# Channel attention and a rational feed-forward layer on one core: numerator in SBUF, whole-tile tail steps, output turned by VectorE

## The chip, the cores and the metric

The kernel runs on one core of a Trainium2 chip. The metric is the device time of one execution in microseconds (us). The engines are named as in the profile: PE is TensorE (matmuls; PEld is its weight load), DVE is VectorE, ACT is ScalarE, POOL is GpSimd, and SP is SyncE, which issues the DMAs. SBUF is the on-chip working memory, PSUM the small memory into which PE writes.

## The reference

Two layers in float32, with B = 4, N = 6080, C = 256 and F = 2048:

```python
qn = q / (norm(q, axis=1) + 1e-6); kn = k / (norm(k, axis=1) + 1e-6)
s = kn.T @ qn / tau                      # 256 x 256 for each batch
a = softmax(s, axis=-1)
x = (v @ a).reshape(24320, 256)
h = x @ w_in                             # 24320 x 2048
P = a0 + a1*h + a2*h**2 + a3*h**3
Q = 1 + abs(b0)*abs(h) + abs(b1)*h**2
out = (P / (Q + 1e-6)) @ w_out           # 24320 x 256
```

## The kernel before, in words

**Tiling.** The 6080 rows of a batch are cut into 12 groups: eleven of 512 rows and one of 448, so 48 groups in all, 44 full ones and 4 of 448. Counted by rows they are 47.5 full groups. The attention matrix is folded into `w_in` once for each batch (`Attn.fuse`), so that a group is `v` times eight weight pieces. The 2048 hidden channels are eight *pairs* of 128, so one group is eight calls of `pair`, and a pair's tile is 128 partitions by 2 x 512 = 1024 float32 elements.

**One pair.** PE computes h into `hx`, a PSUM tile of two banks (three such tiles exist), from high and low float32r parts of `v` and of the weight. Then, in SBUF tiles `d`, `r`, `uu` (names `y` and `kk` in the code):

- the denominator Q goes to `d`. A pair of the form F (lines 804 to 810) takes one ACT step, one DVE step `prod`, another ACT step, and later a POOL step `one` that adds 1. The form U (811 to 823) takes two ACT steps and two POOL steps, `line` and `sum`;
- ACT makes `slope` (826), DVE makes `num1` (828) and `num2` (830). `num2` writes the numerator without a0 **back into `hx` in PSUM**;
- ACT makes `root` (834) and `square` (839), which give r = 1/Q approximately;
- the *tail* runs in two halves of 512 elements (852 to 882). DVE `quot` forms (hx + a0)·r, POOL `again` multiplies it by Q in `d`. In an S pair DVE `last` makes the corrected quotient `g`, which PE multiplies with `w_out` in float32. In an R pair DVE `rest` forms the remainder, POOL `last_pool` turns it into a low part `gl`, and PE multiplies high and low parts in float32r.

In each of the DVE steps `prod`, `num1`, `num2`, `quot`, `rest` and `last`, one of the two tensor operands lies in PSUM (`hx`).

`KIND` (line 51) names the form of each of the eight pairs: the first letter is R or S, the second F or U, the third (P) puts the last step of an R pair on POOL. Before, four pairs are R and four are S.

**One group.** All eight pairs add into one PSUM tile `acc`. `finish` (884) copies it with ACT, turns it with eight PE transposes back into `acc`, copies again with ACT into `orow`, and stores it with one DMA. `values` (740) loads `v` with one DMA, turns it on PE, and splits it into `vhi` (ACT) and `vlo` (DVE).

**Order.** `step` does not issue anything: it hands a step with its engine, its cost and a key (from the tables `LAG` and `TIME`) to `Planner`. The planner plays the schedule through with these costs and emits every engine's instructions in the order that it found. Each engine then runs its queue strictly in that order. The planner knows an argument `port`: a DVE step that carries it, and every POOL step, are taken one after the other. `Attn` gives that argument to its DVE steps on the sums of squares, and `piece` to its late weight steps; `pair` gives it to none.

Beside the groups, the next batch's q and k rows are squared by ACT into `sq` and summed by POOL into `ssq` (24 pieces to a batch), and multiplied on PE.

Of the kernel before, what the change touches and what calls it, by code (L numbers as in the profile page):

```python
# [10 lines left out]
F32 = mybir.dt.float32  # L11
# [9 lines left out]
LAG = {  # L21
    "first": (-23.943, 0.779, 16.152, -2.628, 12.275, -14.299, 0.849, 12.204),
    "second": (64.578, 55.323, 59.143, 56.607, 7.413, 49.338, 52.686, 69.362),
    "line": (11.809, -44.33, -0.798, -23.493, 7.232, -28.691, -20.654, -32.78),
    "prod": (-25.799, -25.066, -7.177, -0.027, 1.503, -30.754, -29.951, -14.021),
    "abs": (22.851, -16.828, -6.381, 4.349, 3.845, 0.375, -1.748, -5.521),
    "slope": (-2.413, -14.175, 23.292, -11.592, 10.064, 22.358, 14.327, 33.823),
    "num1": (102.929, 82.894, 81.158, 62.614, 64.142, 120.209, 89.073, 104.516),
    "num2": (-4.828, -66.826, -23.076, -34.364, -51.549, -56.374, -41.833, -65.959),
    "sum": (4.693, 16.192, 3.118, 9.167, 1.798, 5.734, -2.218, 21.491),  # L30
    "root": (8.815, 1.931, -7.534, -8.44, 11.521, 1.596, -18.294, 11.215),
    "one": (27.21, 31.412, 40.487, 22.316, 24.471, -12.593, 43.293, 5.876),
    "square": (-64.503, -49.599, -58.591, -28.542, -47.268, -42.996, -32.677, -8.585),
    "quot": (40.746, 32.008, 16.16, 51.527, 29.306, 35.7, 39.709, 24.527),
    "again": (-61.355, -87.995, -84.935, -58.616, -91.448, -79.4, -44.502, -69.519),
    "rest": (-17.013, -33.435, -9.224, -61.671, -10.183, -41.213, -23.935, -25.063),
    "last": (-39.442, -40.174, -68.15, -83.691, -21.902, -24.741, -46.676, -44.956),
    "last_pool": (-0.493, -59.623, -7.515, -32.037, 18.764, -45.886, -12.678, -10.454),
    "out": (63.96, 25.995, 31.164, 31.971, 24.821, 19.268, 27.921, 33.051),
    "out_lo": (116.352, 93.718, 68.074, 61.654, 91.315, 121.222, 76.822, 102.449),  # L40
}
TIME = {
    "pair": 6.5, "start": 92.588, "load": 1.191, "softmax": 58.031, "in": 2.437,
    "late_in": -22.444, "out0": -54.096, "out": 7.105, "attn0_0": 31.018, "attn_0": 1.206,
    "attn0": 69.854, "attn": 0.995, "attn1": 94.156, "value": 1.073, "fuse": 5.271,
    "finish": -40.738, "front": 35.456, "front_pace": 13.309, "back": 50.586, "store": 55.554,
    "ahead_pe": 283.994, "ahead_act": 1891641.487, "ahead_dve": 6393007968.0, "ahead_pool": 11581445.34,
# [3 lines left out]
KIND = ("RFP", "SU", "RFP", "SF", "RFP", "SU", "RFP", "SF")  # L51
# [63 lines left out]
class Planner:  # L115
# [5 lines left out]
    HOP = {"PE": 0.25, "ACT": 0.07, "DVE": 0.07, "POOL": 0.07, "SP": 3.5}  # L121
# [39 lines left out]
    def order(self):  # L161
# [55 lines left out]
        while left:  # L217
            for e in ready:
                while busy[e] <= now and ready[e]:
# [55 lines left out]
def tile_channel_attention_rational_ffn(  # L275
# [41 lines left out]
    def apart(eng, ins):  # L317
# [4 lines left out]
        slot, bank = half[0]  # L322
        for other, old in seen.get((slot, 1 - bank), ()):
            if other is not eng:
                tc.declare_no_dep(ins.ins, old.ins, reason="the two use different banks of one tile")
        mine = seen.setdefault((slot, bank), [])
        mine.append((eng, ins))
# [79 lines left out]
    b0, b1 = babs[:, 0:1], babs[:, 1:2]  # L407
    w_in_sb = const.tile([P, NC2, F], F32, name="w_in_sb")
# [331 lines left out]
    def values(G, at, gate=()):  # L740
        b, g = divmod(G, NG)
        base, pn = groups[g]
        n = T * pn
        vst = buf("vst", [P, T, C], F32)
        slot = banks()
        hi, lo = buf("vhi", [P, NC2, GT], F32R), buf("vlo", [P, NC2, GT], F32R)
        fn = lambda: sp.dma_start(vst[:pn], v[b, base : base + pn * T].rearrange("(p t) c -> p t c", t=T))
        step("SP", 1.5, at - 3 * II, fn, gate, [vst])

        def turned():  # L750
            for c in range(NC2):
                for t in range(T):
                    pe.transpose(
                        slot[:, c, t * pn : (t + 1) * pn], vst[:pn, t, c * P : (c + 1) * P], ident[:pn, :pn]
                    )
# [10 lines left out]
    def pair(m, at, vparts, w, acc):  # L766
# [23 lines left out]
        for i in range(2):  # L790
            step("PE", 1.38 * s, at + 0.01 * i, lambda i=i: mm1(i), [whi, wlo, vhi, vlo], [hx.both[i]])

        def mm2(i, w, x, first, last):
            for a, g in zip(w, x):
                for e in range(NC2):
                    pe.matmul(
                        acc[:, e, :n], a[:, W_AT[p] + i, e * P : (e + 1) * P], g[:, :n],
                        start=(first and a is w[0]), stop=(last and a is w[-1]),
                    )
# [4 lines left out]
        if kind[1] == "F":  # L804
            fn = lambda: act.activation(c(kk), c(hx), AF.Abs, scale=b1)
            step("ACT", cost(0.87, 0.25), at + LAG["first"][p], fn, [hx], [kk], rank=at + 1.0)
            fn = lambda: dve.scalar_tensor_tensor(c(d), c(kk), b0, c(hx), op0=ALU.add, op1=ALU.mult)
            step("DVE", cost(1.06, 0.22), at + LAG["prod"][p], fn, [kk, hx], [d], rank=at + 1.0)
            fn = lambda: act.activation(c(d), c(d), AF.Abs)
            step("ACT", cost(0.87, 0.17), at + LAG["abs"][p], fn, [d], [d])  # L810
        else:
            fn = lambda: act.activation(c(d), c(hx), AF.Square)
            step("ACT", cost(0.87, 0.16), at + LAG["first"][p], fn, [hx], [d], rank=at + 1.0)
            fn = lambda: act.activation(c(kk), c(hx), AF.Abs, scale=b0)
            step("ACT", cost(0.87, 0.25), at + LAG["second"][p], fn, [hx], [kk], rank=at + 1.0)
            if kind[1] == "A":
                fn = lambda: act.activation(c(d), c(d), AF.Identity, scale=b1, bias=ONE)
                step("ACT", cost(0.87, 0.27), at + LAG["line"][p], fn, [d], [d])
            else:
                fn = lambda: pool.tensor_scalar(c(d), c(d), b1, ONE, op0=ALU.mult, op1=ALU.add)  # L820
                step("POOL", cost(1.06, 0.07), at + LAG["line"][p], fn, [d], [d])
            fn = lambda: pool.tensor_tensor(c(d), c(d), c(kk), op=ALU.add)
# [147 lines left out]
```

## Time and profile before

| | |
|---|---|
| median of 3 runs | 2693.04 us (2691.68 to 2693.2) |
| profiled execution, its own time | 2693.56 us |
| its span, first to last instruction | 2691.8 us |
| mean granted PE clock | 0.992 |
| PE busy | 2601.5 us, 10304 instructions |
| DVE busy | 2473.1 us, 2911 instructions |
| ACT busy | 2238.9 us, 2285 instructions |
| POOL busy | 2287.1 us, 1725 instructions |
| DMA on q1 | 69168 packets, 108.03 MB |

A row of a group of instructions reads: line, engine, operation, output<-inputs with partitions x elements, count | busy us, mean ns of one | idle time before them. Nearly all rows have line 64, since a helper there issues every operation; the tile names tell them apart. A row of a timeline reads: start and duration in us, engine, operation, and in brackets the idle time before it.

### The profile page before, as it was taken

How to read it: one execution, taken by the hardware profiler on the slowest of the kernel's cores; microseconds unless marked ns; L12 is line 12 of the kernel's file. 1: busy time of each engine (PE TensorE's matmuls, PEld its weight loads, DVE VectorE, ACT ScalarE, POOL GpSimd, SP SyncE). 2: the span in 40 equal slices, each digit the busy share in tenths (PEclk: the TensorE clock that was granted, in tenths of full speed). 3: DMA queues.
4: the chain of work that ended last, by engine and by line, in shares of the span. 5: the costliest groups of instructions: out<-in, count | busy, mean ns of one | idle time of the engine just before them, and what ended most of it. 6: DMA issues, size and time to landing. Idle time of an engine off the chain costs nothing.

```text
span 2691.8 us, 30390 instructions
## 1 busy us (share of the span) xinstructions
PE 2601.5 (97%) x10304; PEld 1864.0 (69%) x10304; DVE 2473.1 (92%) x2911; ACT 2238.9 (83%) x2285; POOL 2287.1 (85%) x1725
## 2 busy tenths in 40 slices
PE   7899999999999999999999999999999999999998
PEld 5766667666766666667777667667777666667666
DVE  8889998899979999998888999999888999999998
ACT  5688887788888888888878888888786888898896
POOL 6598888888768888889978898888996898898897
PEclk9899999999999999999999999999999999999999
DMA  9400002000100000012210000001220000000000
GB/s 318 139 18 16 24 16 85 16 16 31 41 22 16 24 24 16 24 40 77 79 60 15 32 15 17 32 16 47 78 77 24 23 8 24 32 8 24 31 9 15
DMA packets 69324, 109.97 MB, mean 41 GB/s; under 512 B 5296, under 2 KB 53936, under 8 KB 69168
## 3 DMA queue, kind: packets, MB, share of 16 engines
q1 hardware_dynamic: 69168, 108.03, 12.0%
q8 instruction: 81, 1.33, 0.2%
q14 instruction: 75, 0.61, 0.1%
HBM read 83.10 MB, written 24.90 MB: 40 GB/s over the span
## 4 chain that ended last, share of the span: by engine, by line
DVE 38%; PE 33%; POOL 11%; issue 8%; ACT 8%; DMA 1%; SPq 0%; DVEq 0%; POOLq 0%; ACTq 0%
PE hx L64 18%; PE acc L64 15%; DVE hx L64 13%; DVE d L64 9%; DVE uu L64 7%; POOL d L64 7%; DVE g L64 4%; DVE gh L64 3%; ACT uu L64 3%; ACT r L64 2%; POOL gl L64 2%; POOL ssq L64 2%; DVE vlo L64 1%; ACT d L64 1%; POOL orow L64 1%
## 5 line engine op out<-in xcount | busy, mean ns | idle before, releaser
L64 PE MATMUL hx<-vhi,w 128*128 128x512 f32 (+1 forms) x3072 | 1094.5, 413 | 42.4 <-DVE g L64 25.1
L64 PEld LDWEIGHTS hx<-vhi,w 128*128 128x128 f32 x3072 | 578.4, 188 | 240.2 <-DVE g L64 51.8
L64 PE MATMUL acc<-g,w_out_sb 128*128 128x512 f32 (+1 forms) x1536 | 688.9, 587 | 1.1 <-DVE g L64 1.1
L64 POOL TENSOR_TENSOR d<-d,gh 128x512 f32<-128x512 f32 (+1 forms) x384 | 484.2, 1282 | 192.4 <-DVE gh L64 191.9
L64 PE MATMUL hx<-vlo,w 128*128 128x512 f32 (+1 forms) x1536 | 598.5, 390 | 0.0
L64 ACT ACTIVATE uu<-hx,babs 128x1024 f32<-128x1024 f32 (+1 forms) x384 | 423.3, 1102 | 164.9 <-PE hx L64 163.1
L64 POOL TENSOR_TENSOR gl<-d,r 128x512 fp32r<-128x512 f32 (+1 forms) x384 | 489.7, 1283 | 19.9 <-DVE d L64 18.7
L64 DVE SCALAR_TENSOR_TENSOR hx<-uu,coef,hx 128x1024 f32<-128x1024 f32 (+1 forms) x384 | 488.9, 1273 | 3.5
L64 POOL TENSOR_TENSOR d<-d,r 128x512 f32<-128x512 f32 (+1 forms) x384 | 481.3, 1276 | 10.6 <-ACT r L64 8.1
L64 DVE TENSOR_TENSOR uu<-uu,hx 128x1024 f32<-128x1024 f32 (+1 forms) x384 | 461.7, 1202 | 27.8 <-ACT uu L64 27.0
L64 PEld LDWEIGHTS acc<-g,w_out_sb 128*128 128x128 f32 x1536 | 289.9, 189 | 273.1 <-issue 254.7
L64 ACT ACTIVATE uu<-hx,coef 128x1024 f32<-128x1024 f32 (+1 forms) x384 | 457.0, 1190 | 0.0
L64 ACT ACTIVATE r<-d 128x1024 f32<-128x1024 f32 (+1 forms) x384 | 401.9, 1047 | 37.6 <-POOL d L64 34.6
L64 ACT ACTIVATE d<-d 128x1024 f32<-128x1024 f32 (+1 forms) x288 | 301.4, 1047 | 140.7 <-DVE d L64 140.3
L64 ACT ACTIVATE r<-r 128x1024 f32<-128x1024 f32 (+1 forms) x384 | 402.2, 1048 | 5.7
L64 DVE SCALAR_TENSOR_TENSOR d<-uu,babs,hx 128x1024 f32<-128x1024 f32 (+1 forms) x288 | 364.2, 1264 | 29.3 <-ACT uu L64 25.9
L64 POOL TENSOR_SCALAR d<-d,ones 128x1024 f32<-128x1024 f32 (+1 forms) x288 | 322.6, 1120 | 78.0 <-ACT r L64 77.1
L64 PEld LDWEIGHTS hx<-vlo,w 128*128 128x128 f32 x1536 | 290.0, 189 | 72.6 <-issue 26.8
L64 DVE SCALAR_TENSOR_TENSOR d<-hx,coef,d 128x512 f32<-128x512 f32 (+1 forms) x384 | 282.9, 741 | 51.8 <-POOL d L64 51.6
L64 DVE SCALAR_TENSOR_TENSOR hx<-hx,coef,r 128x512 f32<-128x512 f32 (+1 forms) x384 | 288.4, 751 | 22.7 <-ACT r L64 13.4
L64 DVE SCALAR_TENSOR_TENSOR gh<-hx,coef,r 128x512 fp32r<-128x512 f32 (+1 forms) x384 | 269.4, 740 | 23.9 <-ACT r L64 15.4
L64 DVE SCALAR_TENSOR_TENSOR g<-d,hx 128x512 f32<-128x512 f32 (+1 forms) x384 | 257.3, 679 | 20.4 <-POOL d L64 6.5
(101 smaller groups left out, 2990.1 us busy)
## 6 DMA issues: line engine op xcount, KB each, us to landing
vst<-in_v_dram SPq DMA_DIRECT2D x44, 512.0 KB, 3.4
out_dram<-orow SPq DMA_DIRECT2D x44, 512.0 KB, 2.6
kq<-in_k_dram SPq DMA_DIRECT2D x78, 256.0 KB, 3.5
kq<-in_q_dram SPq DMA_DIRECT2D x78, 256.0 KB, 3.8
d<-in_moe_w_in_dram SPq DMA_DIRECT2D x8, 512.0 KB, 6.5
r<-in_k_dram SPq DMA_DIRECT2D x10, 256.0 KB, 6.0
r<-in_q_dram SPq DMA_DIRECT2D x10, 256.0 KB, 6.0
d<-in_moe_w_out_dram SPq DMA_DIRECT2D x4, 512.0 KB, 5.7
```

What stands on the lines that cost most here:

```text
L64: ins = op(*args, **kwargs)
```

## The change

- The numerator: `num2` writes into `y` in SBUF and no longer into `hx`. The steps `quot`, `rest` and `last` then read `y`, and `hx` is released after `num2`.
- The tail runs on the whole tile of 1024 elements: one `quot`, one `again`, one `rest` and one `last` or `last_pool` for a pair, where there were two of each.
- The denominator: a pair of the new form G makes |b1|·h² and |b0|·|h| in two ACT steps (the first with a scale of the root of |b1|, worked out once at the start by `square_root`) and adds them and 1 in one DVE step `prod` whose two tensor inputs are `kk` and `d`. The POOL step `one` and the ACT step `abs` go. A pair of the form A has the step `line` on ACT and `sum` on POOL.
- `KIND`: seven of eight pairs are R (five RGP, two RAP) and one is S (SG).
- The output: `finish` turns `acc` from PSUM into `orow` with one DVE block transpose (32 x 32 blocks) and stores it in four DMAs with runs of 32 elements. The two ACT copies and the eight PE transposes go.
- The rows of `v` come in four DMAs and another row order; they are still turned on PE.
- Slots: `uu` 4 to 5, `w` 9 to 8, `gh` 6 halves to 3 whole tiles, `gl` 4 halves to 2 whole tiles, `g` goes. The planner gets finer costs for the step from one engine to another, and other values of `LAG` and `TIME`.

```diff
-KIND = ("RFP", "SU", "RFP", "SF", "RFP", "SU", "RFP", "SF")
+KIND = ("RGP", "RAP", "RGP", "RGP", "RAP", "RGP", "RGP", "SG")
+VIN = "PE"
+VLO = "DVE"
...
-    SLOTS = {"hA": 3, "hB": 3, "acc": 1, "d": 3, "uu": 4, "r": 3, "gh": 6, "gl": 4, "g": 4, "w": 9, ...
+    SLOTS = {"hA": 3, "hB": 3, "acc": 1, "d": 3, "uu": 5, "r": 3, "gh": 3, "gl": 2, "w": 8, ...
...
+        def put(eng, per, fixed, name, fn, reads, writes, rank=None):
+            step(eng, cost(per, fixed), at + LAG[name][p], fn, reads, writes, rank=None if rank is None else at + rank)
...
+        if kind[1] == "G":
+            fn = lambda: act.activation(c(d), c(hx), AF.Square, scale=b1r)
+            put("ACT", 0.87, 0.25, "first", fn, [hx], [d], 1.0)
+            fn = lambda: act.activation(c(kk), c(hx), AF.Abs, scale=b0)
+            put("ACT", 0.87, 0.25, "second", fn, [hx], [kk], 1.0)
+            fn = lambda: dve.scalar_tensor_tensor(c(d), c(kk), ONE, c(d), op0=ALU.add, op1=ALU.add)
+            put("DVE", 1.06, 0.2, "prod", fn, [kk, d], [d])
...
-        fn = lambda: dve.scalar_tensor_tensor(c(hx), c(y), a1, c(hx), op0=ALU.add, op1=ALU.mult)
+        fn = lambda: dve.scalar_tensor_tensor(c(y), c(y), a1, c(hx), op0=ALU.add, op1=ALU.mult)
...
+        if kind[0] == "S":
+            fn = lambda: pool.tensor_tensor(c(d), c(d), c(r), op=ALU.mult)
+            put("POOL", 2.32, 0.06, "again", fn, [d, r], [d])
+            fn = lambda: dve.scalar_tensor_tensor(c(y), c(y), a0, c(r), op0=ALU.add, op1=ALU.mult)
+            put("DVE", 1.06, 0.2, "quot", fn, [y, r], [y])
+            fn = lambda: dve.scalar_tensor_tensor(
+                c(y), c(d), 2.0, c(y), op0=ALU.subtract, op1=ALU.mult, reverse0=True
+            )
+            put("DVE", 1.06, 0.2, "last", fn, [d, y], [y])
+            fn = lambda: mm2((w_out_sb,), (y,), not old, end)
...
+        fn = lambda: dve.scalar_tensor_tensor(c(ghi), c(y), a0, c(r), op0=ALU.add, op1=ALU.mult)
+        put("DVE", 1.06, 0.2, "quot", fn, [y, r], [ghi], 10.0)
+        fn = lambda: pool.tensor_tensor(c(d), c(d), c(ghi).bitcast(F32), op=ALU.mult)
+        put("POOL", 2.32, 0.06, "again", fn, [d, ghi], [d])
+        fn = lambda: dve.scalar_tensor_tensor(c(y), c(y), a0, c(d), op0=ALU.add, op1=ALU.subtract)
+        put("DVE", 1.06, 0.2, "rest", fn, [y, d], [y])
...
+            fn = lambda: pool.tensor_tensor(c(glo), c(y), c(r), op=ALU.mult)
+            put("POOL", 2.32, 0.06, "last_pool", fn, [y, r], [glo], 10.0)
...
-        step("ACT", 1.05, at, lambda: act.copy(turned[:, :, :n], acc[:, :, :n]), [acc], [turned])
-        step("PE", 1.1, at + TIME["back"], back, [turned], [slot, orow])
-        step("ACT", 1.05, at + TIME["store"], lambda: act.copy(orow[:pn], natural()[:pn]), [slot], [orow])
+        fn = lambda: dve.transpose(natural(), acc[:, :, :n].rearrange("p e (k i) -> p k e i", i=32))
+        step("DVE", 1.28, at, fn, [acc], [orow])
+        dst = out[row : row + n].rearrange("(i k) (e q j) -> q i k e j", k=K, q=4, j=32)
+        def store():
+            for x in range(4):
+                sp.dma_start(dst[x], natural()[32 * x : 32 * x + 32])
```

More of the change, by code (lines that the diff above doesn't have):

```diff
@@ L21 @@
 LAG = {
[L22 to L40, printed above, removed]
+    "first": (-9.95, -5.931, 0.474, 25.318, 8.016, 27.853, 7.02, 46.26),
+    "second": (86.151, 38.43, -4.024, 19.242, 34.472, 66.804, 21.159, 45.832),
@@ L41 @@
+    "out": (14.469, 31.179, 37.299, 25.799, 71.031, 53.51, 40.843, 37.508),
+    "out_lo": (27.001, 35.033, 27.282, 22.651, 25.332, 95.605, 61.008, 63.677),
 }
 TIME = {
[L43 to L46, printed above, removed]
@@ L321, in apart @@
             return
-        slot, bank = half[0]
-        for other, old in seen.get((slot, 1 - bank), ()):
-            if other is not eng:
+        slot, bank, rest = half[0]
+        for other, old, used in seen.get((slot, 1 - bank), ()):
+            if other is not eng and not used & rest:
                 tc.declare_no_dep(ins.ins, old.ins, reason="the two use different banks of one tile")
         mine = seen.setdefault((slot, bank), [])
-        mine.append((eng, ins))
+        mine.append((eng, ins, rest))
         del mine[:-40]
@@ L374, in bank, with step @@
         return Buf(tag, lambda slot: homes["hx"][slot][:, 512 * (tag == "hB") :][:, :512])
-    def step(eng, cost, key, fn, reads=(), writes=(), port=False, rank=None, lone=False):
+    def step(eng, cost, key, fn, reads=(), writes=(), port=False, rank=None):
         new = [b for b in flat(writes) if b.tag is not None and not b.writers]
-        own = {id(b): b for b in (*flat(reads), *flat(writes)) if b.tag in ("hA", "hB")}
+        used = {id(b): b for b in (*flat(reads), *flat(writes))}.values()
+        own = [b for b in used if b.tag in ("hA", "hB")]
+        rest = [b for b in used if b.tag not in ("hA", "hB")]
         def run():
@@ L382, in run @@
                 b.tile = b.view(b.slot)
-            used = {(b.slot, b.tag == "hB") for b in own.values()}
-            half[0] = used.pop() if len(used) == 1 and (eng == "PE" or lone) else None
+            at = {(b.slot, b.tag == "hB") for b in own}
+            if len(at) == 1:
+                half[0] = *at.pop(), {(b.tag, b.slot) if b.tag else id(b) for b in rest}
             fn()
@@ L743, in values @@
         n = T * pn
+        K = n // 32
         vst = buf("vst", [P, T, C], F32)
-        slot = banks()
         hi, lo = buf("vhi", [P, NC2, GT], F32R), buf("vlo", [P, NC2, GT], F32R)
[L747 to L755, printed above, removed]
@@ L761, in values @@
+        fn = lambda: act.activation(hi[:, :, :n], turned[:, :, :n], AF.Copy)
+        step("ACT", 1.05, at + 1, fn, [turned], [hi])
+        e, eng, cost = (dve, "DVE", 1.2) if VLO == "DVE" else (pool, "POOL", 2.38)
+        fn = lambda: e.tensor_tensor(
+            lo[:, :, :n], turned[:, :, :n], hi[:, :, :n].bitcast(F32), op=ALU.subtract
         )
-        step("DVE", 1.2, at + 2, fn, [slot, hi], [lo])
+        step(eng, cost, at + 2, fn, [turned, hi], [lo])
         return hi, lo
@@ L790, in pair @@
         for i in range(2):
[L791 to L799, printed above, removed]
+            step("PE", 1.39 * s, at + 0.01 * i, lambda i=i: mm1(i), [whi, wlo, vhi, vlo], [hx.both[i]])
@@ L801, in cost, with mm2 @@
+        def mm2(w, x, first, last):
+            for i in range(2):
+                for a, g in zip(w, x):
+                    for e in range(NC2):
+                        pe.matmul(
+                            acc[:, e, :n], a[:, W_AT[p] + i, e * P : (e + 1) * P], g[:, i, :n],
+                            start=(first and i == 0 and a is w[0]), stop=(last and i == 1 and a is w[-1]),
+                        )
         def cost(per, fixed):
             return per * s + fixed
[L804 to L810, printed above, removed]
+        def put(eng, per, fixed, name, fn, reads, writes, rank=None):
+            step(eng, cost(per, fixed), at + LAG[name][p], fn, reads, writes, rank=None if rank is None else at + rank)
@@ L835, in pair @@
-        if kind[1] == "F":
-            fn = lambda: pool.tensor_scalar(c(d), c(d), ones[:, 0:1], ONE, op0=ALU.mult, op1=ALU.add)
-            step("POOL", cost(1.06, 0.07), at + LAG["one"][p], fn, [d], [d])
-        fn = lambda: act.activation(c(r), c(r), AF.Square)
-        step("ACT", cost(0.87, 0.2), at + LAG["square"][p], fn, [r], [r])
-        def quot(i, out):
-            dve.scalar_tensor_tensor(out, hx[:, i, :n], a0, r[:, i, :n], op0=ALU.add, op1=ALU.mult)
-        def rest(i, out):
-            dve.scalar_tensor_tensor(out, hx[:, i, :n], a0, d[:, i, :n], op0=ALU.add, op1=ALU.subtract)
@@ new lines, in pair @@
+        put("DVE", 1.06, 0.16, "num1", fn, [y, hx], [y])
+        fn = lambda: dve.scalar_tensor_tensor(c(y), c(y), a1, c(hx), op0=ALU.add, op1=ALU.mult)
+        put("DVE", 1.06, 0.23, "num2", fn, [y, hx], [y])
+        fn = lambda: act.activation(c(r), c(d), AF.Abs_reciprocal_sqrt)
+        put("ACT", 0.87, 0.2, "root", fn, [d], [r], 6.0)
+        fn = lambda: act.activation(c(r), c(r), AF.Square)
+        put("ACT", 0.87, 0.2, "square", fn, [r], [r])
+        old = [acc] if p else []
+        end = p == NFP - 1
@@ new lines, in pair @@
+        if kind[2] == "D":
+            fn = lambda: dve.tensor_tensor(c(glo), c(y), c(r), op=ALU.mult)
+            put("DVE", 1.06, 0.16, "last", fn, [y, r], [glo], 10.0)
+        else:
+            fn = lambda: pool.tensor_tensor(c(glo), c(y), c(r), op=ALU.mult)
+            put("POOL", 2.32, 0.06, "last_pool", fn, [y, r], [glo], 10.0)
+        fn = lambda: mm2((w_out_hi, w_out_lo), (ghi, ghi), not old, False)
+        step("PE", 1.84 * s, at + LAG["out"][p], fn, [ghi, w_out_ok[p], *old], [acc])
@@ L884, in finish @@
+        fn = lambda: mm2((w_out_hi,), (glo,), False, end)
+        step("PE", 0.92 * s, at + LAG["out_lo"][p], fn, [glo, w_out_ok[p], acc], [acc])
     def finish(G, at, acc):
```

152 lines of the change are left out of this document (84 added, 68 removed).

## The prediction

> **What bounds the kernel now.** I read the page's first part, then the stretches of the span, then the groups of instructions by shape, then the timeline where DVE and POOL meet.
>
> ```profile
> span 2691.8 us, 30390 instructions
> PE 2601.5 (97%) x10304; PEld 1864.0 (69%) x10304; DVE 2473.1 (92%) x2911; ACT 2238.9 (83%) x2285; POOL 2287.1 (85%) x1725
> DVE 38%; PE 33%; POOL 11%; issue 8%; ACT 8%; DMA 1%; SPq 0%; DVEq 0%; POOLq 0%; ACTq 0%
> 750.00:1400.00 650.00, 635.45 (x2517) 455.40 (x2517) 593.21 (x688) 544.26 (x549) 565.62 (x425) 0.99 0.11 37
> 2684.57 0.91 ACT L64 COPY orow<-acc 128x896 f32<-128x896 f32 x1 [7.13 <-PE acc L64]
> ```
>
> PE and DVE bound it together: PE is busy 98% of the middle stretch (635 of 650 us), DVE 91%, and the chain that ended last goes through both. POOL, at 85%, carries 11% of the chain. The loop runs from about 100 us to 2684.6 us, when the last `acc` is copied: 2585 us for 47.5 full groups, 54.4 us a group. My sum is made against the profiled execution, 2693.6 us (span and 1.8 us around it), 0.5 us above the median, so nothing is to be corrected.
>
> **The engines' work, before and after.** For a full group, from the rows by shape:
>
> ```profile
> L64 DVE SCALAR_TENSOR_TENSOR hx<-uu,coef,hx 128x1024 f32<-128x1024 f32 x352 | 452.1, 1284 | 3.0
> L64 DVE TENSOR_TENSOR uu<-uu,hx 128x1024 f32<-128x1024 f32 x352 | 427.1, 1213 | 14.5 <-ACT uu L64 13.7
> L64 DVE SCALAR_TENSOR_TENSOR d<-uu,babs,hx 128x1024 f32<-128x1024 f32 x264 | 336.8, 1276 | 25.2 <-ACT uu L64 24.3 <-issue 0.8
> L64 DVE SCALAR_TENSOR_TENSOR hx<-hx,coef,r 128x512 f32<-128x512 f32 x352 | 266.3, 757 | 21.4 <-ACT r L64 13.0 <-ACT uu L64 0.5
> L64 DVE SCALAR_TENSOR_TENSOR d<-hx,coef,d 128x512 f32<-128x512 f32 x352 | 261.2, 747 | 46.6 <-POOL d L64 46.5
> L64 DVE SCALAR_TENSOR_TENSOR gh<-hx,coef,r 128x512 fp32r<-128x512 f32 x352 | 248.6, 746 | 23.4 <-ACT r L64 15.4
> L64 DVE SCALAR_TENSOR_TENSOR g<-d,hx 128x512 f32<-128x512 f32 x352 | 238.0, 684 | 17.6 <-POOL d L64 4.6 <-DVE hx L64 0.5
> L64 DVE TENSOR_TENSOR vlo<-hx,vhi 128x1024 fp32r<-128x1024 f32 x44 | 53.6, 1218 | 3.9 <-ACT vhi L64 3.9
> L64 DVE TENSOR_TENSOR orow<-sq,orow 128x1024 f32<-128x1024 f32 x5 | 6.1, 1219 | 0.0
> L64 POOL TENSOR_TENSOR gl<-d,r 128x512 fp32r<-128x512 f32 x352 | 452.7, 1294 | 14.1 <-DVE d L64 13.7 <-ACT d L64 0.3
> L64 POOL TENSOR_TENSOR d<-d,uu 128x1024 f32<-128x1024 f32 x88 | 211.7, 2406 | 3.4 <-ACT uu L64 0.5
> L64 POOL TENSOR_TENSOR ssq<-sq,ssq 128x1024 f32<-128x1024 f32 x63 | 151.6, 2407 | 35.6 <-ACT sq L64 28.9 <-DVE w L64 6.4
> L64 POOL TENSOR_SCALAR d<-d,ones 128x1024 f32<-128x1024 f32 x264 | 298.0, 1129 | 64.8 <-ACT r L64 63.9
> ```
>
> *DVE before*: prod 6 x 1.276, num1 8 x 1.213, num2 8 x 1.284, 8 halves of quot at 0.757 and 8 at 0.746, rest 8 x 0.747, last 8 x 0.684, vlo 1.218: 52.3 us. *After*: 22 whole-tile steps whose tensor inputs both lie in SBUF (prod 6, quot 8, rest 7, last 1), at the 1.219 us of the row `orow<-sq,orow`, which has that shape and both inputs in SBUF: 26.8 us. Besides, with one input in PSUM: num1 and num2 8 x (1.213 + 1.284), vlo 1.218, and the block transpose, which no row shows. It reads as many elements of PSUM as `num2` does; I take 1.25, between 0.75 (a half-size row) and 2.6 (twice `num2`). That is 22.4 us off the two-input kind, 49.2 in all, 3.1 less.
>
> *POOL before*: 6 adds of 1 (1.129), two `line` like them, two `sum` (2.406), and 24 halves of 1.29: 44.8 us. *After*: eight `again`, seven `last_pool` and two `sum`, 17 whole tiles at 2.406 us: 40.9, so 3.9 less.
>
> ```profile
> 1252.74 0.61 PE L64 MATMUL acc<-gh,w_out_lo 128*128 128x512 f32 x2
> 1253.19 0.62 PE L64 MATMUL acc<-gl,w_out_hi 128*128 128x512 f32 x2
> 1253.65 1.88 PE L64 MATMUL acc<-g,w_out_sb 128*128 128x512 f32 x4
> 2685.52 1.08 PE L64 MATMUL acc<-ident,orow 128*112 128x128 f32 x8 [1.00 <-ACT orow L64]
> L64 ACT ACTIVATE uu<-hx,coef 128x1024 f32<-128x1024 f32 x352 | 422.0, 1199 | 0.0
> L64 ACT ACTIVATE uu<-hx,babs 128x1024 f32<-128x1024 f32 x352 | 391.1, 1111 | 150.1 <-PE hx L64 148.2 <-DVE d L64 0.5
> L64 ACT ACTIVATE r<-r 128x1024 f32<-128x1024 f32 x352 | 371.9, 1057 | 5.4
> L64 ACT COPY orow<-acc 128x1024 f32<-128x1024 f32 x88 | 88.7, 1008 | 1.7 <-PE acc L64 1.7
> ```
>
> *PE*: an R pair's output matmuls are 12 records, 0.45 us for two by their starts (2.7 us); an S pair's are 8 records, 4 in 1.88 less some 0.15 of overlap (3.45 us). Three pairs go from S to R, 2.2 us a group, and the turning back (1.08) goes: 3.3 us of some 53 (98% of 54.4). *ACT* changes abs (1.057) for a second read of PSUM (1.111) in six pairs, takes `line` (about 1.2) in two, and loses two copies (2.02): +0.7 on 47. Off the path while DVE and PE stand at 49 or more.
>
> If nothing else happened, both bounds would fall by 3.1 to 3.3 us, and at today's fill the loop would take 147 us less: 2546 us. The PSUM tiles come free earlier too. So the question is what the 22 steps cost that now read two tensors from SBUF.
>
> **What two SBUF inputs cost beside POOL.** The trace of before has few such steps, but some fall into a POOL instruction:
>
> ```profile
> 81.32 0.67 DVE L64 SCALAR_TENSOR_TENSOR d<-uu,d 128x512 f32<-128x512 f32 x1
> 83.74 2.38 POOL L64 TENSOR_TENSOR ssq<-sq,ssq 128x1024 f32<-128x1024 f32 x1 [15.34 <-ACT sq L64]
> 83.83 2.84 DVE L64 SCALAR_TENSOR_TENSOR w_out_sb<-uu,d 128x512 f32<-128x512 f32 x1
> 99.83 0.67 DVE L64 SCALAR_TENSOR_TENSOR d<-uu,d 128x512 f32<-128x512 f32 x1
> 99.85 2.91 POOL L64 TENSOR_TENSOR ssq<-sq,ssq 128x1024 f32<-128x1024 f32 x1 [1.88 <-ACT sq L64]
> 2028.35 2.33 POOL L64 TENSOR_TENSOR d<-d,gh 128x448 f32<-128x448 f32 x2
> 2030.57 1.21 POOL L64 TENSOR_TENSOR gl<-d,r 128x448 fp32r<-128x448 f32 x1
> 2030.20 2.13 DVE L64 TENSOR_TENSOR ssq<-ssq 128x512 f32<-128x512 f32 x1
> ```
>
> At 83.83 a DVE step that takes 0.67 us alone took 2.84: it began 0.09 us after a POOL instruction that ended at 86.12, and ended at 86.67, 0.55 us later. At 99.83 it is the other way round: DVE came first, and POOL took 2.91 us, ending 2.26 us after DVE's end (100.50). At 2030.20 DVE waited past the end of one POOL instruction (2030.68) and of the next (2031.78), and ended 0.55 us after that. The hot steps of before, with one input in PSUM, show nothing of this: `num2` has a mean of 1.284 with POOL busy 85% of the time. So such a DVE step and a POOL step run one after the other, and a waiting engine saves about 0.13 us of its own start.
>
> The Trainium skill says it as a rule ("SBUF — State Buffer", section "SBUF: two separate sides"): a DVE instruction with two SBUF inputs and a GpSimd instruction that reads SBUF share a port pair as an exclusive lock, held for the whole instruction, and the first to start gets it. By that rule the two engines' full durations add up, the larger sum below; the rows at 83.83 and 99.83 agree with the lock but allow the smaller one. At 2030.20 the row differs from the rule's second half: POOL's next instruction, begun 0.37 us after DVE's, went first.
>
> *The sum of that resource.* Full durations: 17 x 2.406 + 22 x 1.219 = 40.9 + 26.8 = 67.7 us a group. If the engines alternate at each step, 17 x 2.26 + 22 x (1.219 - 0.13 = 1.09) = 62.4. Either is above the 54.4 us that a group takes now; before, only 44.8 us of POOL used it. Over 47.5 groups: 2964 to 3216 us. To it come the `ssq` adds that fall into the loop: 69 are in the trace, 5 begin ahead of the one at 99.85, so 64 x 2.26 to 2.41: 145 to 154 us. Start 100 us, end 10 us (2684.6 to 2693.6, and 1 more).
>
> *When it idles.* The port stands still while POOL has no work and DVE is in one of its PSUM steps (22.4 of 49.2 us, 45%). POOL is without work 15% of the span now; 0.15 x 0.45 = 7% is the upper end, 0 the lower. I take half, since work piles up before a full resource: 3.5% of 3240 is 113 us.
>
> **The other parts.**
>
> ```profile
> q1 hardware_dynamic: 69168, 108.03, 12.0%
> out_dram<-orow SPq DMA_DIRECT2D x4, 448.0 KB, 3.1
> SPq L64 <- PE hx L64: 1288.1, 93, 52.3
> SPq L64 <- ACT orow L64: 1131.4, 48, 51.2
> 2687.68 0.34 SPq L64 DMA_DIRECT2D out_dram<-orow  x1
> L64 DVE TENSOR_SCALAR acc<-d 128x512 uint32<-128x512 uint32 x4 | 2.8, 695 | 5.0 <-DMA d<-in_moe_w_in_dram 4.9
> ```
>
> A packet takes 0.12 x 16 x 2691.8 / 69168 = 0.075 us of one DMA engine. The stores now have runs of 128 bytes, 4096 for a group, at that price 19 us on 16 engines: hidden under a group, and `orow` has two buffers. Only the last store shows: 3584 runs, 17 us in place of 3.1, +14; with bytes as the price, 0. I take 8. SP issues eight DMAs a group where it had two; it waits 2420 us for others now, so they cost nothing, and what is queued behind a store (the next `v` and the q and k rows) waits for DVE's transpose where it waited for ACT's copy. Without that slack, six issues of 0.34 us would cost 2.0 us a group. `square_root` is seven tiny DVE steps at the start, where DVE waits 4.9 us for the first DMA; three more split weights cost DVE and ACT some 2 us each before the loop. Taken at 0, at most 5 us.
>
> **The sum.** Mean of both port sums, 3090, and `ssq` 150, idle 113, ends 110, last store 8: **3470 us**. Its own range: 2964 + 145 + 110 = 3219, to 3216 + 154 + 236 (7% of 3370) + 118 = 3724.
>
> **Rivals.**
> *B, the tiles bound it:* three `r` tiles are held from `root` to `last_pool`: 1.06 + 1.06 + 1.22 + 2.41 + 1.22 + 2.41 = 9.4 us, and four steps that may each wait 2.4 us for the port: 19 us, 6.3 us a pair over three tiles, below the port's 8.1. But queues run in a fixed order, planned as if the port were free, so a stalled DVE step holds up `num1` and `num2` of later pairs. With ten more us of this a tile lives 29 us: 9.7 us a pair, 77.3 a group, 3673 + 150 + 118 = 3940 us. For it: DVE and POOL wait for each other in each R pair four times. Against: work for other pairs fills the waits now. 0.12.
>
> *C, faster:* the whole-tile steps mostly find POOL idle or are not held up. Then 2546 us as above. It decides if a DVE step holds the port for less than (54.4 - 38.4 - 3.1 for `ssq`) / 22 = 0.59 us in place of 1.09. Against it is each row above in which the two meet. 0.06.
>
> *D, one side pays:* DVE waits for POOL, but POOL hardly for DVE. DVE's 49.2 us less 0.09 of overlap for each of 40 records, 45.6, and 22 waits of half a POOL step (1.2 us) in the 62% of time when POOL is busy, 16.4: 62 us, 2945 + 110, and some 100 for `ssq`, 3160 us. The row at 99.85 speaks against it; that POOL got in first at 2030.57, for it. 0.11.
>
> **How the numbers follow.** My forecast has 0.70; B 0.12, C 0.06, D 0.11, and 0.01 for a time within 0.2% of before, which is about what a measurement of this kernel can tell. So faster 0.06, same 0.01, slower 0.93. The range leaves out C, B's upper part and a little of D: 3130 to 3780.
>
> **What would show it.** In the profile after, the all-SBUF DVE steps should have means far above 1.22 us (near 2) with a minimum of 1.2, while `num1` and `num2` stay at 1.21 and 1.28; POOL's whole-tile steps should come to 2.4 to 3.2 us; the recorded busy shares of DVE and POOL should be high, since waits lie inside the records; PE should fall to about 70 to 75% with idle time released by DVE. The stores should show some 195,000 packets without being on the chain. If `quot` and `prod` show 1.2 us while POOL is busy, I am wrong and C holds. If their sum per group is near 65 us but the group takes 77, it is B.

## The result and the profile after

The changed kernel takes 3491.64 us (median; 3490.57 to 3494.39) against 2693.03 before: 1.297 times as long, 95% interval 1.2946 to 1.2991. The profiled execution spans 3488.7 us. The forecast was 3470, with 3219 to 3724 as its own range.

The first part of the page of after and the stretch of the windows view that was shown of before (us; busy us of PE, PEld, DVE, ACT, POOL with instructions; PE clock, DMA share, GB/s):

```profile
span 3488.7 us, 28950 instructions
PE 2732.0 (78%) x10496; PEld 2098.6 (60%) x10496; DVE 3395.6 (97%) x2200; ACT 2268.2 (65%) x2287; POOL 2579.3 (74%) x909
DVE 67%; issue 17%; PE 9%; POOL 4%; ACT 1%; DMA 1%; SPq 0%; POOLq 0%; DVEq 0%; ACTq 0%
750.00:1400.00 650.00, 518.09 (x1999) 395.68 (x1998) 644.62 (x417) 432.29 (x439) 475.05 (x167) 0.91 0.10 21
q1 hardware_dynamic: 262320, 108.04, 12.5%
```

DVE is recorded as busy for 97% of the span although it has a quarter fewer instructions (2200 for 2911). PE has gone from 98% to 80% of the middle stretch. Whoever takes DVE's share at its word would call DVE overloaded; the groups by shape say otherwise:

```profile
L64 DVE SCALAR_TENSOR_TENSOR uu<-uu,coef,d 128x1024 f32<-128x1024 f32 x308 | 679.2, 2205 | 20.3 <-POOL d L64 19.9
L64 DVE SCALAR_TENSOR_TENSOR gh<-uu,coef,r 128x1024 fp32r<-128x1024 f32 x308 | 642.2, 2093 | 7.0 <-ACT r L64 3.7 <-DVE uu L64 0.5
L64 DVE SCALAR_TENSOR_TENSOR d<-uu,d 128x1024 f32<-128x1024 f32 x264 | 603.1, 2285 | 10.2 <-ACT d L64 6.5 <-ACT uu L64 3.6
L64 DVE SCALAR_TENSOR_TENSOR uu<-uu,coef,hx 128x1024 f32<-128x1024 f32 x352 | 446.7, 1270 | 2.2
L64 DVE TENSOR_TENSOR uu<-uu,hx 128x1024 f32<-128x1024 f32 x352 | 424.7, 1208 | 0.0
L64 DVE SCALAR_TENSOR_TENSOR uu<-uu,coef,r 128x1024 f32<-128x1024 f32 x44 | 138.1, 3139 | 0.4
L64 DVE SCALAR_TENSOR_TENSOR uu<-d,uu 128x1024 f32<-128x1024 f32 x44 | 104.3, 2370 | 0.2
L64 DVE STREAM_TRANSPOSE orow<-acc 128x1024 f32<-128x1024 f32 x44 | 54.7, 1244 | 4.7 <-PE acc L64 4.4
L64 POOL TENSOR_TENSOR d<-d,gh 128x1024 f32<-128x1024 f32 x308 | 889.8, 2893 | 383.2 <-DVE gh L64 383.2
L64 POOL TENSOR_TENSOR gl<-uu,r 128x1024 fp32r<-128x1024 f32 x308 | 878.3, 2852 | 356.2 <-DVE uu L64 305.3 <-PE acc L64 42.5 <-PE hx L64 2.5
```

The steps with `hx` (PSUM) among their inputs stay at 1.208 and 1.270 us, and the transpose out of PSUM takes 1.244. The five kinds with two SBUF inputs have means of 2.09 to 3.14. Their busy time for the 44 full groups is 2166.9 us, 49.2 a group, where 22 steps of 1.219 are 26.8: 22.4 us of each group are waits that lie inside the records. POOL's two commonest steps go from 2.41 to 2.89 and 2.85 us. DVE's idle column shows almost nothing: its wait for this resource does not appear as idle time. POOL does stand idle, 739 us before these two steps, mostly for DVE's results, so its busy share falls.

A stretch of the timeline of after, DVE and then POOL, shows how the records interlock:

```profile
2048.70 1.27 DVE L64 SCALAR_TENSOR_TENSOR uu<-uu,coef,hx 128x1024 f32<-128x1024 f32 x1
2049.90 2.23 DVE L64 SCALAR_TENSOR_TENSOR uu<-uu,coef,d 128x1024 f32<-128x1024 f32 x1
2052.05 1.27 DVE L64 SCALAR_TENSOR_TENSOR gh<-uu,coef,r 128x1024 fp32r<-128x1024 f32 x1
2053.25 1.21 DVE L64 TENSOR_TENSOR uu<-uu,hx 128x1024 f32<-128x1024 f32 x1
2054.38 2.27 DVE L64 SCALAR_TENSOR_TENSOR d<-uu,d 128x1024 f32<-128x1024 f32 x1
...
2047.66 3.38 POOL L64 TENSOR_TENSOR gl<-uu,r 128x1024 fp32r<-128x1024 f32 x1
2052.27 3.30 POOL L64 TENSOR_TENSOR gl<-uu,r 128x1024 fp32r<-128x1024 f32 x1 [1.23 <-DVE uu L64]
2055.53 3.41 POOL L64 TENSOR_TENSOR d<-d,gh 128x1024 f32<-128x1024 f32 x1
```

At 2049.90 `rest` waits for POOL's instruction that ends at 2051.04 and ends 1.09 us after it. At 2052.27 POOL waits for the `quot` that ends at 2053.32, and ends 2.25 us after that. `num1` at 2053.25 runs beside POOL in its normal 1.21 us.

### The profile page after: what moved, and what is told of

It is laid out like the page before. It is cut to its first block, busy times and chain, and to the rows that moved or that the text cites. A ratio compares the mean times of both kernels' runs of the same rounds, so it can differ in the third digit from the quotient of the medians.

```text
span 3488.7 us, 28950 instructions
## 1 busy us (share of the span) xinstructions
PE 2732.0 (78%) x10496; PEld 2098.6 (60%) x10496; DVE 3395.6 (97%) x2200; ACT 2268.2 (65%) x2287; POOL 2579.3 (74%) x909
## 3 DMA queue, kind: packets, MB, share of 16 engines
q1 hardware_dynamic: 262320, 108.04, 12.5%
q8 instruction: 83, 1.36, 0.2%
## 4 chain that ended last, share of the span: by engine, by line
DVE 67%; issue 17%; PE 9%; POOL 4%; ACT 1%; DMA 1%; SPq 0%; POOLq 0%; DVEq 0%; ACTq 0%
DVE uu L64 35%; DVE gh L64 14%; DVE d L64 12%; PE hx L64 6%; PE acc L64 3%; POOL d L64 2%; DVE orow L64 2%; DVE vlo L64 1%; POOL orow L64 1%; POOL gl L64 1%; POOL ssq L64 0%; DVE hx L64 0%; ACT r L64 0%; DVE w L64 0%; ACT d L64 0%
## 5 line engine op out<-in xcount | busy, mean ns | idle before, releaser
L64 POOL TENSOR_TENSOR d<-d,gh 128x1024 f32<-128x1024 f32 (+1 forms) x336 | 957.4, 2853 | 427.3 <-DVE gh L64 423.5
L64 POOL TENSOR_TENSOR gl<-uu,r 128x1024 fp32r<-128x1024 f32 (+1 forms) x336 | 947.3, 2820 | 390.5 <-DVE uu L64 326.8
L64 DVE SCALAR_TENSOR_TENSOR uu<-uu,coef,d 128x1024 f32<-128x1024 f32 (+1 forms) x336 | 732.3, 2179 | 23.4 <-POOL d L64 23.0
L64 DVE SCALAR_TENSOR_TENSOR gh<-uu,coef,r 128x1024 fp32r<-128x1024 f32 (+1 forms) x336 | 685.9, 2049 | 7.4 <-ACT r L64 3.7
L64 DVE SCALAR_TENSOR_TENSOR d<-uu,d 128x1024 f32<-128x1024 f32 (+2 forms) x295 | 650.2, 2204 | 14.2 <-ACT d L64 10.4
L64 ACT ACTIVATE d<-hx,broot 128x1024 f32<-128x1024 f32 (+1 forms) x288 | 317.9, 1105 | 259.8 <-DVE uu L64 222.6
L64 DVE SCALAR_TENSOR_TENSOR uu<-uu,coef,hx 128x1024 f32<-128x1024 f32 (+1 forms) x384 | 483.3, 1259 | 2.7
L64 PE MATMUL acc<-gh,w_out_hi 128*128 128x512 f32 (+1 forms) x1344 | 428.9, 401 | 20.9 <-DVE orow L64 20.9
L64 PE MATMUL acc<-gl,w_out_hi 128*128 128x512 f32 (+1 forms) x1344 | 392.9, 416 | 64.9 <-POOL gl L64 64.7
L64 PE MATMUL acc<-gh,w_out_lo 128*128 128x512 f32 (+1 forms) x1344 | 418.5, 393 | 0.0
```

The costliest lines, as they stand in the source:

```text
L64: ins = op(*args, **kwargs)
```

## The experiments

In the expectations, "lock theory" is the prediction's main case: a DVE step with two SBUF inputs and a POOL step that reads SBUF run one after the other. What they share is called the port. The code under each heading is cut to the lines that matter.

**The disputed steps alone.** Nothing of the reference is computed; 16 steps on each engine in each stretch.

```diff
+    SECTIONS = [
+        (stt, None), (None, tt), (stt_psum, None), (turn, None),
+        (stt, tt), (stt_psum, tt), (turn, tt), (stt, ts), (stt, fill),
+        (halves(stt), halves(tt)), (mix, tt),
+    ]
```

> Only the disputed steps: eleven stretches of 16 steps of 1024 elements on DVE, on POOL or on both at once; the output is zeros. Lock theory: DVE with two SBUF inputs alone 1.13 us from start to start, POOL's tensor_tensor alone 2.4; both at once take 16 x (2.26 + 1.09) = 54 us, not the 38.5 of the slower one. DVE with one PSUM input, and the block transpose out of PSUM (about 1.25 us), beside the same POOL steps: 38.5 us. Beside POOL's tensor_scalar (1.13): 16 x (1.0 + 1.09) = 33 us, not 18. Beside a POOL memset, which reads nothing: by the lock as the page has it no stall. In halves of 512: again the sum, about 55 to 58 us. One two-SBUF and one PSUM step in turn beside POOL: 54 us, the PSUM step hidden under POOL. Rival (no lock, the long records of after come from something else in the kernel): each double stretch takes as long as the slower engine alone.

Its timeline, each stretch of 16 merged into one row (start, duration); the order is each engine alone, both with two SBUF inputs, the short copy that DVE makes behind that stretch, DVE from PSUM beside POOL, POOL's one-input step beside DVE, and DVE beside POOL's memset:

```profile
5.47 21.10 DVE L22 SCALAR_TENSOR_TENSOR do<-da,go,db 128x1024 f32<-128x1024 f32 x16
27.43 38.59 POOL L22 TENSOR_TENSOR po<-pa,pb 128x1024 f32<-128x1024 f32 x16
109.87 50.47 DVE L22 SCALAR_TENSOR_TENSOR do<-da,go,db 128x1024 f32<-128x1024 f32 x16
109.96 52.57 POOL L22 TENSOR_TENSOR po<-pa,pb 128x1024 f32<-128x1024 f32 x16
160.37 2.19 DVE L22 COPY tok<-do 128x4 f32<-128x4 f32 x1
163.26 21.08 DVE L22 SCALAR_TENSOR_TENSOR do<-px,go,db 128x1024 f32<-128x1024 f32 x16
163.35 38.66 POOL L22 TENSOR_TENSOR po<-pa,pb 128x1024 f32<-128x1024 f32 x16
242.30 33.00 POOL L22 TENSOR_SCALAR po<-pa,go 128x1024 f32<-128x1024 f32 x16
276.03 21.10 DVE L22 SCALAR_TENSOR_TENSOR do<-da,go,db 128x1024 f32<-128x1024 f32 x16
276.10 16.08 POOL L22 MEMSET po<- 128x1024 f32 x16
```

Both together take 52.57 us, where the slower alone takes 38.59; with one input in PSUM each runs as if alone. A POOL step with one SBUF input blocks too (33.0 us), a memset, which reads nothing, does not (21.10 and 16.08). In halves of 512 the pair of streams took 53.49 us, so small steps do not help; alternating two-SBUF and PSUM steps took 52.68. One whole step of each costs 52.57 / 16 = 3.29 us. The Trainium skill ("SBUF — State Buffer", section "SBUF: two separate sides") names the pair of conditions, two SBUF inputs on DVE against a GpSimd step that reads SBUF, and these rows of DVE's two-input steps agree with it.

Two inputs are not the only case that waits. The short DVE copy behind each stretch has one SBUF input and takes 0.17 us when POOL is idle; at 160.37, with POOL's last step still running until 162.53, it took 2.19. So did a one-input step of before: at 87.38 a DVE TENSOR_SCALAR took 1.91 us beside POOL's step that ended at 89.01, and one like it took 0.42 at 94.41, with POOL idle. The change adds no such step to the loop.

**The same instructions without POOL's hold.** POOL's 17 tail steps of a group are cut to 64 columns, so most of those products are left out.

```diff
-        fn = lambda: pool.tensor_tensor(c(d), c(d), c(ghi).bitcast(F32), op=ALU.mult)
+        fn = lambda: pool.tensor_tensor(d[:, :, :64], d[:, :, :64], ghi[:, :, :64].bitcast(F32), op=ALU.mult)
... (the other three POOL steps likewise)
```

> After, with POOL's 17 tail steps of a group cut to 64 of their columns (the rest of those products is left out; gl is filled once at the start). DVE, PE and ACT do all that they did. Lock theory: the two-SBUF DVE steps come down to 1.22 us and the time to DVE's own 49 us a group and its fill: 2450 to 2650 us. Rival (a shorter chain is what helps, or DVE slowed by something else than POOL): the DVE steps keep means near 2 us and the time stays above 3000.

2532.95 us, 0.94 of before, inside the range of the lock theory. The groups of DVE in this run:

```profile
L64 DVE SCALAR_TENSOR_TENSOR uu<-uu,coef,d 128x1024 f32<-128x1024 f32 x308 | 418.2, 1358 | 0.7 <-POOL d L64 0.7
L64 DVE SCALAR_TENSOR_TENSOR gh<-uu,coef,r 128x1024 fp32r<-128x1024 f32 x308 | 406.8, 1329 | 6.5 <-ACT r L64 3.3 <-PE acc L64 0.2
L64 DVE SCALAR_TENSOR_TENSOR d<-uu,d 128x1024 f32<-128x1024 f32 x264 | 344.4, 1304 | 9.9 <-ACT uu L64 5.4 <-ACT d L64 4.2
```

DVE's instructions are those of after; their means fall from 2.1 to 2.3 us to 1.30 to 1.36 once POOL holds the port only briefly. The run takes most of POOL's work away as well (POOL is busy 867 us, 2579 in after), so its time does not tell the port from the shorter chain; the means do, for DVE's records, and how much of the 959 us is the port's is not separated here.

**One part of the change at a time, on before.** The numerator alone:

```diff
-        fn = lambda: dve.scalar_tensor_tensor(c(hx), c(y), a1, c(hx), op0=ALU.add, op1=ALU.mult)
+        fn = lambda: dve.scalar_tensor_tensor(c(y), c(y), a1, c(hx), op0=ALU.add, op1=ALU.mult)
...
-            dve.scalar_tensor_tensor(out, hx[:, i, :n], a0, r[:, i, :n], op0=ALU.add, op1=ALU.mult)
+            dve.scalar_tensor_tensor(out, y[:, i, :n], a0, r[:, i, :n], op0=ALU.add, op1=ALU.mult)
... (rest and last likewise; uu 5 slots, w 8)
```

> Before, with the numerator alone kept in SBUF (five uu slots, eight w slots); tails in halves, four S pairs, old denominator and old output. Lock theory: 32 half steps with two SBUF inputs, 0.56 to 0.69 us, join POOL's 40.4 to 44.8 us a group: 58 to 67 us, with ssq, the ends and 3.5% idle some 3330 us (3100 to 3450). Rival (the whole-tile tail, the longer chain through three d and r tiles, costs the time): 2650 to 2720, since the halves are kept.

3462.96 us (1.2857 times before, 1.2836 to 1.2879). This one part by itself costs 770 us, nearly as much as the whole change, with tails in halves and the old output. Its four rows of half steps, now with two SBUF inputs:

```profile
L64 DVE SCALAR_TENSOR_TENSOR uu<-uu,coef,r 128x512 f32<-128x512 f32 x352 | 524.9, 1518 | 19.0 <-ACT r L64 18.8
L64 DVE SCALAR_TENSOR_TENSOR d<-uu,coef,d 128x512 f32<-128x512 f32 x352 | 490.4, 1404 | 25.2 <-POOL d L64 23.8
L64 DVE SCALAR_TENSOR_TENSOR gh<-uu,coef,r 128x512 fp32r<-128x512 f32 x352 | 415.6, 1203 | 14.4 <-ACT r L64 10.6 <-DMA kq<-in_q_dram 0.7 <-PE acc L64 0.7
L64 DVE SCALAR_TENSOR_TENSOR g<-d,uu 128x512 f32<-128x512 f32 x352 | 382.2, 1098 | 0.6
```

They take 1813.1 us together where the same steps took 1014.1 from PSUM: 799 us more in DVE's records, for 770 us of time. The run lies 133 us above the 3330 and 13 above the range given. In its trace the port, counted as the time in which a POOL step or a two-input DVE step is recorded, stands empty for 10% of the loop (from 100 us to 10 us before the end), where the expectation had put in 3.5%.

The denominator alone, six steps a group with two SBUF inputs:

```diff
-            fn = lambda: dve.scalar_tensor_tensor(c(d), c(kk), b0, c(hx), op0=ALU.add, op1=ALU.mult)
+            fn = lambda: dve.scalar_tensor_tensor(c(d), c(kk), ONE, c(d), op0=ALU.add, op1=ALU.add)
```

> Before, with the denominator alone summed in one DVE step with two SBUF inputs (six pairs of a group). Lock theory: 6 x 1.09 to 1.22 us join a POOL that has lost 6.8 us a group, 41 to 45 us in all, below the period: the port isn't full, each such step waits half a POOL half-step or so: 2700 to 2900 us. Rival without a lock: POOL and ACT have less to do and DVE the same: 2650 to 2700.

2871.99 us (1.0663, 1.0647 to 1.0679): slower although POOL lost a sixth of its instructions, and inside the range of the lock theory. `prod` has a mean of 1.617 us for 1.276, and POOL's half steps 1.42 to 1.47 for 1.29.

The input and output part alone:

```diff
-        step("ACT", 1.05, at, lambda: act.copy(turned[:, :, :n], acc[:, :, :n]), [acc], [turned])
-        step("PE", 1.1, at + TIME["back"], back, [turned], [slot, orow])
-        step("ACT", 1.05, at + TIME["store"], lambda: act.copy(orow[:pn], natural()[:pn]), [slot], [orow])
+        fn = lambda: dve.transpose(natural(), acc[:, :, :n].rearrange("p e (k i) -> p k e i", i=32))
... (four stores for one, and the new row order of v)
```

> Before, with the input and output part alone: v in four DMAs and the other row order, output turned by DVE from PSUM, four stores in runs of 128 bytes. If the loss of after is all the port's: 2650 to 2760 us (PE loses 1.08 us a group, ACT 2.0, DVE gains 1.25). Rival (the transpose or the small stores carry a good part of the 800 us): above 2800.

2784.12 us (1.034, 1.0324 to 1.0355), between the two cases given. DVE's busy time rises by 59 us (2532.4 for 2473.1), which is 47.5 transposes of 1.25; DVE was one of the two bounds. PE's weight loads for `acc` wait 92.4 us for the transpose. Which share of the 91 us is the output's and which that of the new loads of `v` was not separated.

Whole-tile tails alone, and seven R pairs alone:

```diff
-        for i in range(2):
+        fn = lambda: dve.scalar_tensor_tensor(c(ghi), c(hx), a0, c(r), op0=ALU.add, op1=ALU.mult)
... (one quot, again, rest or last, and last_pool for 1024 elements; the next lines are the other run)
-KIND = ("RFP", "SU", "RFP", "SF", "RFP", "SU", "RFP", "SF")
+KIND = ("RFP", "RUP", "RFP", "RFP", "RFP", "RUP", "RFP", "SF")
```

> Before, with whole-tile tails alone (one quot, again, rest or last for a pair; numerator in PSUM, four S pairs, old denominator and output). No step has two SBUF inputs, so by the lock alone nothing is lost: 2650 to 2720 us. But after with numerator and denominator put back still took 2932 us, 239 above before, of which the output part accounts for 91: if whole tiles, which give hx back to PE only when the whole pair is done, are the rest, 2780 to 2880. Rival (the seven R pairs are the rest): 2650 to 2720 here.

> Before, with seven R pairs and one S pair alone (halves kept, numerator in PSUM; the forms of the denominator kept; w slots 8). PE loses 2.2 us a group, POOL gains six half steps of 1.29: 52.5 us and ssq 3.3, 55.8 us a group, more than the 54.4 of now. If POOL becomes the bound: 2750 to 2880. If whole tiles are what is left unexplained: 2650 to 2750.

2833.85 us (1.0522, 1.0508 to 1.0537) and 2945.34 us (1.0936, 1.0921 to 1.0951). Neither has a step of the loop with two SBUF inputs. The first came out where its expectation put it if whole tiles were the rest; the second lies above both of its ranges. With whole tiles DVE's busy time even falls, to 2400 us, while the span grows by 142: no engine is full (PE has 93%), so waits between them take the time. That `hx` comes back later is one explanation. The waits fit it, though no run tried it by itself: PE's matmuls into `hx` wait 78.7 us for `last` (26.2 before), ACT 217.9 us for `hx` (163.1), and `prod` 150.1 us for ACT (25.9). With seven R pairs POOL reaches 90%.

**Parts taken back out of after.** The numerator in PSUM, the old denominator, and both:

```diff
-        fn = lambda: dve.scalar_tensor_tensor(c(y), c(y), a1, c(hx), op0=ALU.add, op1=ALU.mult)
+        fn = lambda: dve.scalar_tensor_tensor(c(hx), c(y), a1, c(hx), op0=ALU.add, op1=ALU.mult)
... (quot, rest and last read hx; the next lines are the old denominator; the third run has both)
-KIND = ("RGP", "RAP", "RGP", "RGP", "RAP", "RGP", "RGP", "SG")
+KIND = ("RFP", "RAP", "RFP", "RFP", "RAP", "RFP", "RFP", "SF")
```

> After, with the numerator alone put back into PSUM (num2 writes hx; quot, rest and last read hx; rest writes y). Everything else as after, the denominator's step with two SBUF inputs too. Lock theory: 6 DVE steps of 1.09 to 1.22 us and POOL's 17 of 2.26 to 2.41, 45 to 48 us a group, with ssq 48 to 51, beside DVE's 49: 55 to 62 us a group, 2700 to 3050 us. Rival (whole-tile tails and their longer chain, or the output part): 3300 or more stays.

> After, with the old denominator alone (form F: prod reads PSUM, POOL adds the 1); the numerator stays in SBUF. Six locked DVE steps go, six POOL steps of 1.13 us come: 17 x 2.26 to 2.41 + 6 x 1.0 to 1.13 + 16 x 1.09 to 1.22 = 62 to 67 us a group, as much as after (62.4 to 67.7): 3300 to 3520 us by the lock. Rival (the price goes with the number of two-input DVE steps, 22 to 16): 3270.

> After, with the numerator in PSUM and the old denominator (form F, the one-input POOL step back): no DVE step of the loop has two SBUF inputs; whole-tile tails, seven R pairs and the new output stay. Lock theory: POOL 17 x 2.406 + 6 x 1.13 = 47.7 and ssq 3.3, 51 us a group, is the bound, DVE 49, PE 50: at today's fill 54 to 56 us, 2600 to 2750 us. Rival (chain length through three tiles): above 2900.

| | denominator G (two SBUF inputs) | denominator F (one in PSUM) |
|---|---|---|
| numerator in SBUF | 3491.6 (after) | 3360.6 |
| numerator in PSUM | 3174.4 | 2932.1 |

`after_old_den` came out as the sum of the port said, 3360.6 in 3300 to 3520. The other two missed their ranges, by 124 and 182 us above the upper ends, and the last one lies where its rival put it (above 2900). Counted as above, the port stands empty for 2.4% of the loop with the old denominator and 5.5% in after, but for 23% with the numerator in PSUM: there its sum is no longer the bound. With both put back no step is held up:

```profile
L66 DVE SCALAR_TENSOR_TENSOR gh<-hx,coef,r 128x1024 fp32r<-128x1024 f32 x308 | 394.1, 1280 | 56.0 <-ACT r L66 46.2
L66 POOL TENSOR_TENSOR d<-d,gh 128x1024 f32<-128x1024 f32 x308 | 738.3, 2401 | 104.8 <-DVE gh L66 100.4
```

DVE, POOL and PE are busy 84, 83 and 88%: no engine is full. So 559 us of after go, net, with its 22 two-input steps (3491.6 less 2932.1), and 239 with the rest of the change once the numerator is back in PSUM. The three other parts alone cost 91, 140 and 252 us on before; they add up to 483, not 239, and how they share it stays open. The longer chain through three tiles, the rival, is one candidate that no run took by itself.

**The order.** Only the planner is told of the port; DVE's instructions are the same in number, in another order.

```diff
+            port = eng == "DVE" and name in ("prod", "quot", "rest", "last")
... (handed to `step`)
```

> After, where only the planner is told that prod, quot, rest and last share the port with POOL; the same instructions in another order. Lock theory with the order as a side issue: the port's sum (62.4 to 67.7 us a group) stays: 3230 to 3520 us. Rival (the order, made for a free port, costs most of the time): below 3000.

3492.81 us, the time of after. An order made with the port known to the planner, the tables left as they are, wins nothing.

**A try at a better version.** One more R pair on before:

```diff
-KIND = ("RFP", "SU", "RFP", "SF", "RFP", "SU", "RFP", "SF")
+KIND = ("RFP", "SU", "RFP", "RFP", "RFP", "SU", "RFP", "SF")
```

> A try at a better version: before, with one S pair (the fourth) made an R pair. PE loses 0.72 us a group (34 us in all), POOL gains 2.6 (47.4 and ssq 3.3, 50.7 of 54.4), DVE is unchanged. If PE is what the fill hangs on: 2650 to 2680. If DVE and POOL are: 2690 to 2740.

2985.18 us (1.1083, 1.1068 to 1.1098): slower than with seven R pairs, and outside both cases. No engine is full (PE 90, DVE 83, POOL 81%), and ACT's wait for PE's `hx` grows from 163.1 to 484.2 us. The tables of due times were not made for this pair; whether that is the cause was not tried. If it is, it bears on the other runs with one part changed as well, which also keep the tables of the kernel they start from: the 91, 140 and 252 us, and the 239, may hold some of it. No kernel with the full computation was faster than before.

## Why the prediction was right, point by point

**The lock and its price.** The row at 83.83 of before, one DVE step of 2.84 us for 0.67, carried the forecast, and the alone run confirms both its forms: a whole-tile DVE step that waited ends 1.08 us after POOL's step, where 1.09 had been worked out, and POOL's ends 2.20 us after DVE's, where 2.26 had been read off; in after they are 1.09 and 2.25. By the alone run a group's 17 POOL steps, each in turn with a DVE step, and 5 more DVE steps are 17 x 3.29 + 5 x 1.22 = 62.0 us, about the lower of the two sums (62.4).

**The sum a group.** The chain that ended last repeats in the final batch, where no `ssq` adds run:

```profile
3197.76 6.91 DVE uu L64 x4
3266.00 6.91 DVE uu L64 x4
3334.27 6.91 DVE uu L64 x4
3402.53 6.89 DVE uu L64 x4
```

One group takes 68.3 us; predicted were 65.05 (the mean of the two sums) and 3.5% of idle, 67.4. In the records from 3197.76 to 3402.53 a POOL step or a two-input DVE step is under way for 64.0 us of a group (2 us above the alone run's sum), and neither for 4.3 us, which is 6.3%. So the good agreement has some luck in it: the port's sum was taken 1 us too high, and its idle share, a half taken between 0 and 7% without a measurement, is nearly twice the 3.5%, though inside those bounds. 47.5 x 68.3 = 3244 for the loop, against 3090 + 113 = 3203.

**The other terms.** The rest, 3489 - 3244 = 245 us, answers to 150 + 118 = 268 predicted for `ssq`, start and end; it was not taken apart. The transpose was taken at 1.25 and took 1.244. The last store was over-sized: the small runs brought 193,000 more packets, yet the share of the DMA engines is 12.5% of 3489 us for 12.0% of 2692, some 0.009 us for each added packet, and the stores land after a median of 3.3 us. From the issue of the last store to the end of the span it is 6.0 us, 4.1 before: its 8 us should have been about 2.

**The rivals.** C is refuted by each row above; a time near its 2546 comes only with most of POOL's work left out (2533). D is refuted by POOL's 2.85 to 2.89 us for 2.41: both sides pay. B's price (3940, 77.3 us a group) did not come; that its mechanism, tiles that are held longer, has no part in the port's idle 6.3% is not shown, and the runs without the lock (2833.9, 2932.1) show that waits outside the port weigh in this kernel too; the prediction's sum has no term for them but the port's idle time. "What would show it" held but for two things: POOL's share fell (74%), since POOL waits idle for DVE's results, and PE kept 78%, above the 70 to 75% named.

**A part not seen.** The prediction put all of the change beside the lock at a gain of 147 us. No run shows it: 2533 comes with most of POOL's work left out, and with the numerator in PSUM the output part, the whole tiles and the seven R pairs each cost time on before's tables. It made little difference to the forecast, because the port bounded the sum.

## What to carry to other kernels

Before moving an operand from PSUM to SBUF, count for each DVE step how many of its tensor inputs then lie in SBUF, and add the hold of those with two to the work of every POOL instruction that reads SBUF: if that sum passes the period (the time of one group), it is a lower bound of the new one, whatever the engines' own loads say (62.0 of 68.3 us here). Below the period the collisions still cost: with the denominator alone the sum was 41 to 45 of 54.4 us, and the time rose by 179 us. DVE's one-input steps from SBUF belong on the list to look at, since short ones waited here too. One or two stray collisions in a trace are enough to see it: look for a rare instruction whose longest record is its normal one plus a POOL instruction. A wait of this kind sits inside the records, so the records of both engines grow, and the idle column of the engine that is never short of work stays empty.

## What the runs showed that had not been expected

PE runs slower after a long wait. In after the mean granted clock is 0.904 (0.992 before). Its rows hold 1.0 or 0.5; one microsecond after a PE wait of 3 us or longer it is 0.5 in 107 of 112 cases, after a wait of 1 to 2 us in 3 of 41. Twelve matmuls into `hx` on the chain that ended last, which followed a wait of 4.38 us, take 4.87 us at a mean clock of 0.59:

```profile
3352.38 4.87 PE hx L64 x12
```

Twelve such matmuls on the chain of before, at a clock of 1.00:

```profile
2596.67 2.74 PE hx L64 x12
```

So a kernel bound elsewhere shows a slower PE as a consequence. As far as the waits show, it costs little here: DVE waits 9.3 us in all for PE's `acc`, and ACT's steps into `uu` and `d` wait 169 us for PE's `hx`, where they waited 177 before. In the run with POOL's steps cut to 64 columns the clock is back at 0.996.

With nothing held up at the port, the change with its numerator in PSUM and the old denominator takes 2932 us, and with the numerator in SBUF and POOL's steps cut to 64 columns 2533. Whether a numerator in SBUF would pay if it met no POOL step, because `hx` comes free sooner, cannot be read from these two: POOL's work differs too. No run has both the SBUF numerator and a full POOL without collisions.
